# A gated linear-attention and token-mixing block: the last modulation vector summed by a chain of accumulating DMAs, two others folded into one matmul each, one projection reordered, a longer tail bank

## The chip, the cores and the metric

The kernel runs on one core of a Trainium2 chip. A core has five engines that run their own queues of instructions: TensorE (PE in the profile; its weight loads are PEld), VectorE (DVE), ScalarE (ACT), GpSimd (POOL) and SyncE (SP). DMAs are issued by an engine and carried by 16 DMA engines. The metric is the device time of one execution in microseconds. The kernel before takes 440.69 us, the median of three runs (440.43 to 441.95).

## The reference, cut to what matters

S = 2048 tokens, D = 448 channels, 16 heads of 28, F = 1792.

```python
mod = (silu(c) @ w_mod).reshape(1, 6, 1, D)
sa, ca, ga, sb, cb, gb = six vectors of mod          # j = 0 .. 5 in the kernel
h = layernorm(x) * (1 + ca) + sa
q, k, v = split(h @ wqkv);  phi(t) = where(t > 0, t + 1, exp(t)) + 1e-6
kv = sum over tokens of phi(k) v^T per head;  z = sum of phi(k)
o = (phi(q) kv) / (phi(q) z + 1e-6)
x = x + ga * (o @ wo)
h = layernorm(x) * (1 + cb) + sb
u = gelu(h^T @ w1 + b1);  y = (u @ w2 + b2)^T
x = x + gb * y
```

All is float32. The six modulation vectors are each a sum over the 448 inputs of c, held as 4 chunks of 112 rows (G = 112): vector j is the sum over the rows k of silu(c)[k] * w_mod[k, j*448:(j+1)*448], and it is used as a tile of 128 equal rows.

## The kernel before, in words

Everything is tiled by 128 tokens (16 tiles, t = 0 .. 15). Matmul operands in float32 are split into a high part, which the matmul takes exactly, and a low part; a product is then three matmuls (high by high, high by low, low by high), written into one accumulating bank of PSUM. The function `split` makes the two: ScalarE copies the high part (L79), VectorE subtracts (L80). In other places the low part is made by ScalarE, which writes the negative high part, and by an accumulating DMA on POOL, which adds the full value (L226, L404, L432, L257).

The order of every engine's work is written out by hand: the program order of the Python text is the order on each engine's queue, and semaphores make an instruction wait for its data or its buffer.

- **Stage A**, the loop over t = 3 .. 15 (L594): key projection of tile t (`project`, L356), transposes of tile t + 1 (L325), the outer products of tile t - 3 into four banks (`a_outer`, L453), and on the other engines the layer norm and its modulation (L307, L313), exponentials, phi and the splits of tiles ahead. Tiles 0 to 2 are done by hand ahead of the loop (L501 to L590). The query projection of tile 1, `project(1, 0, "qp", True)` (L582), sorts its eleven products by the key on L353, so that products with the low parts of the weight come late: high by high (3), low by high (3), low weights (3), then the two of the short fourth chunk. The low part of the first weight chunk is made by a DMA (`w_low_dma`, L226).
- **Between the stages** (L652 to L852): the sums, the products of kv with wo (L846), and the first splits of w1.
- **Stage B**, the loop over i = 0 .. 20 (L855): transposes of the normalised queries (L758), output projection (L778), residual, second layer norm, and from i = 5 the first products with w1 (`step`, L828 to L830). POOL makes small statistics there (L736, L792, L806, L811, L813, L818).
- **The last part** (from L1117): the remaining products with w1, gelu, and the products with w2 in a seven-product scheme (L1028, L1029); stores of the output.

The modulation vectors are made in three ways. Vectors 0 and 1 are done at the start and aren't touched here. Vectors 2, 4, 3 and 5 go through `load_mod` (four loads by SP), `mod_part` (VectorE multiplies a chunk by its column of silu(c) and adds it to an accumulator of 112 rows, L181 and L183; for vector 5 the first chunk is done by ScalarE, L179), `mod_split` (high and low part, 112 rows each), `mod_sum2` (two matmuls with a block of ones sum the rows and repeat the result in 128 rows, L199 and L200) and `mod_out` (ScalarE copies the bank out, L161). Their places: vector 2 has its products at t = 5 .. 8, the split at t = 9, the matmuls at t = 10 (L602), and it scales wo at t = 11 .. 14 (L611). Vector 4 has its products at t = 11 .. 14 and vector 3 at t = 15 and behind the loop; both are split at L670 and L671 and summed at L686 and L697. Vector 5 is loaded at i = 12 of stage B (L857), its products run at i = 13 .. 15, its matmuls stand at i = 16 (L868) and it is used from L945 and L1155 on.

At the very end, `mult7` leaves the last LAST = 2 row blocks of the last product out of their bank and hands them to `last7` (L1038), which multiplies them into a bank of its own (L1043) while VectorE adds the closed bank to the result (L1045); the last add takes the new bank, and SP stores the tile (L1046).

Buffers of 128 rows by 2 KB come from a pool of 76 (`slot`), and others from a pool of 25 that ends with stage B (`tslot`); a new tile waits for the last readers of the one whose buffer it gets.

Of the kernel before, what the change touches and what calls it, by code (L numbers as in the profile page):

```python
# [8 lines left out]
F32 = mybir.dt.float32  # L9
F32R = mybir.dt.float32r  # L10
AF = mybir.ActivationFunctionType
ALU = mybir.AluOpType
AX = mybir.AxisListType

P = 128
# [15 lines left out]
DVE_LOW = (0, 1, 13, 14, 15)  # L31
AHEAD = 8
LAG = 5
LAST = 2
PRE2 = {16: (1, 0), 12: (1, 1), 8: (1, 2), 3: (4, 3), 1: (4, 4)}
MOD_AT = {11: [(4, 0)], 12: [(4, 1)], 13: [(4, 2)], 14: [(4, 3)], 15: [(3, 0), (3, 1)]}
QS = {0: 2, 4: 2}
WARM = 9
ACT_STATS = ()
PRE = 9  # L40
# [7 lines left out]
def block_kernel(ctx: ExitStack, tc: tile.TileContext, x, wqkv, wo, w1, b1, w2, b2, c, wmod, out):  # L48
# [23 lines left out]
    def moving(new, name, dt=F32R, parts=P):  # L72
        return new(name, dt=dt, parts=parts, w=512)[:, 16:16 + D]

    def bank(name):
        return psum.tile([P, 512], F32, name=name, tag="bank")
# [32 lines left out]

    def load_mod(j):  # L110
        for k in range(4):
            wm[j, k] = (tslot if j == 5 else slot)(f"wm{j}_{k}", parts=G)
            nc.sync.dma_start(wm[j, k], wmod[k * G:(k + 1) * G, j * D:(j + 1) * D])

    raw_w = {}
# [38 lines left out]
    nc.vector.tensor_scalar_add(ec, ec, 1.0)  # L154
    nc.vector.reciprocal(ec, ec)
    nc.vector.tensor_mul(sc, ct, ec)
    mods, macc, part = {}, {}, {}

    def mod_out(j, ps):
        mods[j] = cst.tile([P, D], F32, name=f"mod{j}")  # L160
        nc.scalar.activation(mods[j], ps[:, :D], AF.Copy, bias=1.0 if j in (1, 4) else 0.0)  # L161
# [26 lines left out]
        return ps  # L188


    def mod_split(j):
        acc = macc.pop(j)
        macc[j] = (moving(slot, f"mh{j}", parts=G), moving(slot, f"ml{j}", parts=G))
        split(acc, *macc[j])

    def mod_sum2(j):
        ps = bank(f"modp{j}")
        hi, lo = macc.pop(j)
        nc.tensor.matmul(ps[:, :D], ones_r[:G, :], hi, start=True, stop=False)  # L199
        nc.tensor.matmul(ps[:, :D], ones_r[:G, :], lo, start=False, stop=True)  # L200
        return ps

    Whi, Wlo = {}, {}

# [31 lines left out]
    def load_to(i):  # L236
        while done["load"] < min(i, len(pieces)):
            k = done["load"]
            src, r, c0, n = pieces[k]
            raws[k] = slot(f"pr{k}", 4 * P)  # L240
            rows = 1 if n == 4 else 2
            nc.sync.dma_start(raws[k].rearrange("p (r c) -> p r c", r=rows),
                              src[r * P:(r + rows) * P, c0 * P:(c0 + n) * P].rearrange("(r p) c -> p r c", p=P))
            done["load"] += 1

    def split_to(i):
        while done["split"] < min(i, len(pieces)):
            k = done["split"]
            if k in TOKP:
                hi, lo = tslot(f"ph{k}", F32R, w=4 * P), tslot(f"pl{k}", F32R, w=4 * P)  # L250
            else:
                hi, lo = slot(f"ph{k}", 4 * P, F32R), slot(f"pl{k}", 4 * P, F32R)
            if k in PIECE_DMA:
                full = raws.pop(k)
                nc.scalar.activation(hi, full, AF.Copy)
                nc.scalar.activation(lo, hi.bitcast(F32), AF.Copy, scale=-1.0)
                nc.gpsimd.dma_start(lo, full, accum_op=ALU.add)  # L257
            else:
                split(raws.pop(k), hi, lo)
            parts[k] = (hi, lo)  # L260
            done["split"] += 1
# [81 lines left out]
    def project(t, j, name, late_low=False):  # L343
        hh, hl = heads[t]
        ps = bank(f"{name}{t}")
        o = ps[:, :D]
        todo = []
        for ch in range(4):
            a, b = (hh, ch, Whi[j, ch]), (hl, ch, Whi[j, ch])
            todo += [a, b] if ch == 3 else [a, (hh, ch, Wlo[j, ch]), b]  # L350
        if late_low:
            ws = [Wlo[j, ch] for ch in range(3)]
            key = lambda m: 3 if m[1] == 3 else 2 if any(m[2] is w for w in ws) else 0 if m[0] is hh else 1  # L353
            todo.sort(key=key)
        for n, (a, ch, b) in enumerate(todo):
            nc.tensor.matmul(o, a[:, ch * P:(ch + 1) * P], b, start=(n == 0), stop=(n == 10))  # L356
        return o
# [236 lines left out]
    for t in range(3, NT):  # L594
        kp = project(t, 1, "kp")
        if t + 1 < NT:
            a_transpose(t + 1)
        a_outer(t - KV_LAG)
        if t in Q_EARLY:
            a_q(t)  # L600
        if t == 10:
            mp = mod_sum2(2)  # L602
        if t + 1 < NT:
            a_split(t + 1)
        if t + 2 < NT:
            a_norm_a(t + 2)

        for j, i in MOD_AT.get(t, ()):
            mod_part(j, i)
        if 11 <= t < 15:  # L610
            nc.vector.tensor_mul(wo_sb[t - 11], wo_sb[t - 11], mods[2][:G])  # L611
        a_exp(t, kp)
        if t + 2 < NT:
            a_norm_b(t + 2)
        a_pk(t, kp)
        a_phi_q()
        a_pk_parts(t - 1)
        if t + 3 < NT:
            a_stats(t + 3)
        if t + 2 < NT:  # L620
            a_dup(t + 2)
        if t == 3:
            a_high(3)
            a_high(4)
        if t + 2 < NT:
            a_high(t + 2)
        if t == 10:
            mod_out(2, mp)
        if t + 4 < NT:
            load_x(t + 4)  # L630
        if 5 <= t < 9:
            mod_part(2, t - 5)
        if t == 9:
            mod_split(2)
        if 5 <= t <= 5 + QLATE:
            phi_q_sum(t - 5)
        if t in (10, 11):
            load_mod(14 - t)
        if t == 4:
            for g in range(4):  # L640
                w = tslot(f"wo{g}", parts=G)
                nc.sync.dma_start(w, wo[g * G:(g + 1) * G, :])
                wo_sb.append(w)
            load_qkv(2, tslot)
            b1c = cst.tile([P, NF], F32, name="b1c")
            nc.sync.dma_start(b1c, b1.rearrange("(k p) -> p k", p=P))
            b2c = cst.tile([P, NT], F32, name="b2c")
            nc.sync.dma_start(b2c, b2.rearrange("(k p) -> p k", p=P))
        load_to(PRE_LOAD.get(t, 0))
# [20 lines left out]
    mod_split(4)  # L670
    mod_split(3)  # L671
    load_to(14)
    split_to(4)
    zb = tslot("zb")
    nc.scalar.activation(zb, zp[:, :D], AF.Copy, bias=S * 1e-6)
# [18 lines left out]
    kvm = slot("kvm", parts=G)  # L694
    nc.vector.tensor_mul(kvm, kvb[:G, :D], mask)
    mod_out(4, mp)
    mp = mod_sum2(3)  # L697
    load_to(PRE + MID + 3)
    split_to(8)
# [144 lines left out]
    for g in range(4):  # L844
# [5 lines left out]
        Wph.append(hi)  # L850
        Wpl.append(lo)
    mod_out(3, mp)  # L852

    accs, early = None, []
    for i in range(NT + LAG):  # L855
        if i == NT - 4:
            load_mod(5)  # L857
        if NT - 3 <= i < NT:
            mod_part(5, i - NT + 3)
        if i < NT:  # L860
            b_transpose(i)
        if 0 <= i - 1 < NT:
            b_out(i - 1)
        nq = min(len(late), QS.get(i, 1))
        for _ in range(nq):
            a_q(late.pop(0))
        t = i - LAG
        mp = mod_sum2(5) if i == NT else None  # L868
        if t >= 0:
            if t == 0:  # L870
                accs = [bank(f"up{f}") for f in range(4)]
            if i > NT:
                if not early:
                    early = [bank(f"up{W1G[1][0] + f}") for f in range(W1G[1][1])]
                r = i - NT - 1
                step(NT + r, early, H2h[r], H2l[r], r == 0, False)
            step(t, accs, H2h[t], H2l[t], t == 0, t == NT - 1)
        if mp is not None:
            mod_out(5, mp)
        scale, res, norm1, norm2 = i + 1 < NT, 0 <= i - 2 < NT, 0 <= i - 3 < NT, 0 <= i - 4 < NT  # L880
        if i < NT:
            b_high(i)
        if res:
            b_res(i - 2)
        if scale:
            b_prod(i + 1)
        if norm2:
            b_norm2(i - 4, i)
        if res:
            b_mean1(i - 2, i)  # L890
        if norm1:
            b_norm1_a(i - 3)
        if scale:
            b_sum(i + 1)
        if norm1:
            b_norm1_b(i - 3, i)
        if scale:
            b_eps(i + 1)
        if i < NT:
            b_low(i)  # L900
        if norm1:
            b_mean2(i - 3, i)
        if scale:
            b_recip(i + 1)
        if scale:
            b_scale(i + 1)
        if scale:
            b_dup(i + 1)
        if norm2:
            b_low2(i - 4)  # L910
        a_phi_q(nq)
        load_to(14 + (i + 1) // 2)
        if res or norm1:
            b_rstd(i, 0 if res else 1, 2 if norm1 else 1)
        if i == NT - 1:
            mod_part(5, 3)
            mod_split(5)
        split_to(10 + (i + 1) // 2)


# [291 lines left out]
```

## Time and profile before

| | us |
|---|---|
| median of three runs | 440.69 |
| the profiled execution | 440.77 |
| its span, first to last instruction | 439.1 |
| busy time of POOL | 119.3 |
| software DMAs (POOL's queue), share of 16 engines | 23.8% |

The page gives the busy time of each engine, then the span in 40 slices of 11 us, the DMA queues, the chain of work that ended last, the costliest groups of instructions, and the DMA issues. Rows of the timeline give the start, the duration, the engine, the line, and in brackets how long the engine had been idle and what ended that. Two rows of the slices show how the load is spread (tenths busy):

```profile
DVE  5996898988898999997469586439999998898894
DMA  8987999993441224222427546476667977977531
```

VectorE is at nine tenths in many slices of the first half; the DMA engines are close to full in the first nine slices, which are stage A.

### The profile page before, as it was taken

How to read it: one execution, taken by the hardware profiler on the slowest of the kernel's cores; microseconds unless marked ns; L12 is line 12 of the kernel's file. 1: busy time of each engine (PE TensorE's matmuls, PEld its weight loads, DVE VectorE, ACT ScalarE, POOL GpSimd, SP SyncE). 2: the span in 40 equal slices, each digit the busy share in tenths (PEclk: the TensorE clock that was granted, in tenths of full speed). 3: DMA queues.
4: the chain of work that ended last, by engine and by line, in shares of the span. 5: the costliest groups of instructions: out<-in, count | busy, mean ns of one | idle time of the engine just before them, and what ended most of it. 6: DMA issues, size and time to landing. Idle time of an engine off the chain costs nothing.

```text
span 439.1 us, 7288 instructions
## 1 busy us (share of the span) xinstructions
PE 433.9 (99%) x2394; PEld 402.4 (92%) x2394; DVE 365.1 (83%) x792; ACT 266.9 (61%) x570; POOL 119.3 (27%) x196
## 2 busy tenths in 40 slices
PE   8999999999999999999999999999999999999996
PEld 7689999999899999999999999999999999999996
DVE  5996898988898999997469586439999998898894
ACT  3778877655657777776766254236675555655550
POOL 2205775520024455664300000010112230231110
PEclk9999999999999999999999999999999999999999
DMA  8987999993441224222427546476667977977531
GB/s 233 303 213 117 181 197 230 221 258 102 138 100 26 47 47 123 50 50 60 132 69 237 177 143 186 131 194 187 151 143 191 177 172 176 188 161 208 75 52 34
DMA packets 65022, 64.51 MB, mean 147 GB/s; under 512 B 8472, under 2 KB 56792, under 8 KB 64984
## 3 DMA queue, kind: packets, MB, share of 16 engines
q1 hardware_dynamic: 54608, 47.62, 36.8%
q0 software_dynamic: 10368, 16.42, 23.8%
q8 instruction: 19, 0.31, 0.3%
q14 instruction: 19, 0.16, 0.1%
q10 hardware_dynamic: 8, 0.00, 0.0%
HBM read 41.88 MB, written 7.34 MB: 112 GB/s over the span
## 4 chain that ended last, share of the span: by engine, by line
PE 95%; DMA 3%; DVE 1%; ACT 0%; issue 0%; SPq 0%; DVEq 0%
PE y L1028 19%; PE up L829 10%; PE up L828 10%; PE up L830 10%; PE y L1029 9%; PE op L778 8%; PE cacc L453 8%; PE qp L356 7%; PE kp L356 7%; DMA wl<-wr 2%; PE tq L758 2%; PE tp L325 1%; DMA wm<-in_w_mod_dram 1%; PE kvb L691 1%; PE wp L846 1%; PE colp L475 0%
## 5 line engine op out<-in xcount | busy, mean ns | idle before, releaser
L829 PE MATMUL up<-h2l,ph 128*128 128x448 f32 x224 | 81.3, 363 | 0.0
L828 PE MATMUL up<-h2h,ph 128*128 128x448 f32 x224 | 81.2, 362 | 0.0
L830 PE MATMUL up<-h2h,pl 128*128 128x448 f32 x224 | 80.7, 360 | 0.0
L988 POOL DMA_DIRECT2D a<-a x16 | 14.1, 948 | 145.5 <-DMA a<-in_B_w_dram 97.8
L828 PEld LDWEIGHTS up<-h2h,ph 128*128 128x128 f32 x224 | 42.0, 188 | 3.3
L830 PEld LDWEIGHTS up<-h2h,pl 128*128 128x128 f32 x224 | 41.9, 187 | 3.0
L829 PEld LDWEIGHTS up<-h2l,ph 128*128 128x128 f32 x224 | 42.0, 188 | 2.1
L80 DVE TENSOR_TENSOR pl<-pr,ph 128x512 fp32r<-128x512 f32 x48 | 32.3, 686 | 11.5 <-ACT ph L79 8.6
L79 ACT ACTIVATE ph<-pr 128x512 fp32r<-128x512 f32 x48 | 29.1, 627 | 17.8 <-PE up L829 7.4
L1050 ACT ACTIVATE cc<-y 128x448 f32<-128x448 f32 x24 | 13.0, 544 | 22.9 <-PE y L1029 22.9
L453 PE MATMUL cacc<-pkh,xh 128*128 128x448 f32 x64 | 24.3, 379 | 0.0
L453 PE MATMUL cacc<-pkl,xh 128*128 128x448 f32 x64 | 23.2, 363 | 0.0
L778 PE MATMUL op<-oh,pth 128*128 128x448 f32 x60 | 23.0, 383 | 0.0
L1071 POOL DMA_DIRECT2D out_dram<-yt x14 | 12.9, 921 | 34.9 <-DVE yt L1057 25.4
L778 PE MATMUL op<-oh,ptl 128*128 128x448 f32 x60 | 21.7, 362 | 0.0
L356 PE MATMUL qp<-wh,hh 128*128 128x448 f32 x60 | 21.6, 365 | 0.0
L356 PE MATMUL qp<-wh,hl 128*128 128x448 f32 x60 | 21.4, 362 | 0.0
L356 PE MATMUL kp<-wh,hl 128*128 128x448 f32 x56 | 20.3, 363 | 0.0
L356 PE MATMUL kp<-wh,hh 128*128 128x448 f32 x56 | 20.2, 362 | 0.0
L736 POOL TENSOR_SCALAR den<-den 128x16 f32<-128x16 f32 x16 | 8.6, 536 | 39.2 <-DVE den L733 39.1
L763 ACT ACTIVATE pth<-tq 128x512 fp32r<-128x512 f32 (+1 forms) x16 | 9.6, 599 | 15.7 <-PE tq L758 15.6
L302 POOL TENSOR_TENSOR rs<-ve,mhalf 128x1 f32<-128x1 f32 x16 | 13.9, 869 | 18.8 <-DVE ve L300 18.5
(234 smaller groups left out, 1356.9 us busy)
## 6 DMA issues: line engine op xcount, KB each, us to landing
pr<-in_B_w_dram SPq DMA_DIRECT2D x56, 256.0 KB, 2.9
a<-in_B_w_dram SPq DMA_DIRECT2D x32, 256.0 KB, 4.3
a<-in_B_w_dram SPq DMA_DIRECT2D x32, 192.0 KB, 4.2
wm<-in_w_mod_dram SPq DMA_DIRECT2D x24, 196.0 KB, 4.9
x<-in_A_x_dram SPq DMA_DIRECT2D x16, 224.0 KB, 4.0
out_dram<-x SPq DMA_DIRECT2D x14, 224.0 KB, 2.0
out_dram<-yt POOLq DMA_DIRECT2D x14, 224.0 KB, 4.5
pk<-pk POOLq DMA_DIRECT2D x12, 224.0 KB, 4.7
```

Source lines behind the costliest of these rows:

```text
L79: nc.scalar.activation(hi, full, AF.Copy)
L80: nc.vector.tensor_sub(lo, full, hi.bitcast(F32))
L302: nc.gpsimd.tensor_tensor(rs, ve, mhalf[:, 0:1], op=ALU.pow)
L356: nc.tensor.matmul(o, a[:, ch * P:(ch + 1) * P], b, start=(n == 0), stop=(n == 10))
L453: nc.tensor.matmul(cacc[ch][:, :D], a[:, s], b, start=(t == 0 and i == 0), stop=(t == NT - 1 and i == len(todo) - 1))
L778: nc.tensor.matmul(opb[t][:, :D], a[:, g * P:(g + 1) * P], b, start=(n == 0), stop=(n == len(todo) - 1))
L828: nc.tensor.matmul(ps[:, :D], hi[:, sl], mh, start=first, stop=False)
L829: nc.tensor.matmul(ps[:, :D], hi[:, sl], ml, start=False, stop=False)
L830: nc.tensor.matmul(ps[:, :D], lo[:, sl], mh, start=False, stop=last)
L988: nc.gpsimd.dma_start(w, a, accum_op=ALU.add)
L1028: nc.tensor.matmul(ps[:, :D], h[:, s], w, start=opens and r == r0, stop=False, skip_group_check=True)
L1029: nc.tensor.matmul(ps[:, :HD], l[:, s], wh, start=False, stop=closes and r == PAIRS - 1 - (LAST if (q, m) == (NP - 1, 6) else 0), skip_gro ...
```

## The change

- **Vector 5** is no longer summed by PE. Its four chunks are loaded at t = 12 of stage A into buffers of the pool of 76, scaled in place by ScalarE at t = 14 and 15, added to one chunk by three accumulating DMAs on POOL, and that chunk's 112 rows are folded onto themselves by seven more (112 to 56, 28, 14, 7, 4, 2 and 1 rows; `mod_fold`). The one row goes to DRAM by SP at i = 9 (`mod_row`) and comes back repeated in 128 rows at i = 10 (`mod_rows`). The products, the split, the two matmuls and the copy out of i = 12 .. 16 are gone.
- **Vectors 2 and 4** are folded before they are split: an accumulating DMA on POOL adds rows 64 to 111 of the accumulator to rows 0 to 47 (`fold`, at the end of t = 8 for vector 2, and at t = 14 for vector 4). High and low part of the 64 rows then lie in one tile of 128 rows, and one matmul with the ones sums both. For vector 2 the split moves from t = 9 to t = 10, the matmul and the copy out from t = 10 to 11, and the scalings of wo from t = 11 .. 14 to 12 .. 15.
- **The query projection of tile 1** takes the product with the low part of weight chunk 0 as the last of its eleven.
- **LAST** goes from 2 to 3.

```diff
-LAST = 2
+LAST = 3
+FOLD_AT = {3: 28, 4: 14, 5: 7, 6: 4, 7: 2}
+FOLDED = (2, 4)
...
+    def fold(j):
+        nc.gpsimd.dma_start(macc[j][:G - 64], macc[j][64:], accum_op=ALU.add)
+
     def mod_split(j):
         acc = macc.pop(j)
+        if j in FOLDED:
+            macc[j] = moving(slot, f"mb{j}")
+            split(acc[:64], macc[j][:64], macc[j][64:])
+            return
...
     def mod_sum2(j):
         ps = bank(f"modp{j}")
+        if j in FOLDED:
+            nc.tensor.matmul(ps[:, :D], ones_r, macc.pop(j), start=True, stop=True)
+            return ps
...
+    def mod_fold(j, n):
+        acc = macc[j]
+        h = (n + 1) // 2
+        nc.gpsimd.dma_start(acc[:n - h], acc[h:n], accum_op=ALU.add)
+
+    def mod_row(j):
+        mrow[j] = park.tile([1, D], F32, name=f"mrow{j}")
+        nc.sync.dma_start(mrow[j], macc.pop(j)[:1])
+
+    def mod_rows(j):
+        mods[j] = cst.tile([P, D], F32, name=f"mod{j}")
+        nc.sync.dma_start(mods[j], mrow[j].to_broadcast([P, D]))
...
-            key = lambda m: 3 if m[1] == 3 else 2 if any(m[2] is w for w in ws) else 0 if m[0] is hh else 1
+            key = lambda m: 3 if m[1] == 3 else 4 if m[2] is ws[0] else 2 if any(m[2] is w for w in ws) else 0 if m[0] is hh else 1
...
-        if t == 10:
+        if t == 11:
             mp = mod_sum2(2)
...
+        if t == 14:
+            fold(4)
-        if 11 <= t < 15:
-            nc.vector.tensor_mul(wo_sb[t - 11], wo_sb[t - 11], mods[2][:G])
+        if 12 <= t < 16:
+            nc.vector.tensor_mul(wo_sb[t - 12], wo_sb[t - 12], mods[2][:G])
...
-        if t == 10:
+        if t == 11:
             mod_out(2, mp)
...
-        if t == 9:
+        if t == 8:
+            fold(2)
+        if t == 10:
             mod_split(2)
...
+        if t == 12:
+            load_mod(5)
+        if t in (14, 15):
+            for k in (2 * t - 28, 2 * t - 27):
+                nc.scalar.activation(wm[5, k], wm[5, k], AF.Copy, scale=sc[:, k:k + 1])
+        if t == 15:
+            for k in range(2):
+                nc.gpsimd.dma_start(wm[5, k], wm[5, k + 2], accum_op=ALU.add)
...
     load_to(14)
+    nc.gpsimd.dma_start(wm[5, 0], wm[5, 1], accum_op=ALU.add)
+    macc[5] = wm[5, 0]
     split_to(4)
...
     mod_out(4, mp)
+    mod_fold(5, G)
...
     mod_out(3, mp)
+    mod_fold(5, 56)
...
     for i in range(NT + LAG):
-        if i == NT - 4:
-            load_mod(5)
-        if NT - 3 <= i < NT:
-            mod_part(5, i - NT + 3)
...
-        mp = mod_sum2(5) if i == NT else None
...
-        if mp is not None:
-            mod_out(5, mp)
...
+        if i in FOLD_AT:
+            mod_fold(5, FOLD_AT[i])
+        if i == 9:
+            mod_row(5)
+        if i == 10:
+            mod_rows(5)
...
-        if i == NT - 1:
-            mod_part(5, 3)
-            mod_split(5)
```

More of the change, by code (lines that the diff above doesn't have):

```diff
@@ L111, in load_mod @@
         for k in range(4):
-            wm[j, k] = (tslot if j == 5 else slot)(f"wm{j}_{k}", parts=G)
+            wm[j, k] = slot(f"wm{j}_{k}", parts=G)
             nc.sync.dma_start(wm[j, k], wmod[k * G:(k + 1) * G, j * D:(j + 1) * D])
@@ L156, in block_kernel @@
     nc.vector.tensor_mul(sc, ct, ec)
-    mods, macc, part = {}, {}, {}
+    mods, macc, part, mrow = {}, {}, {}, {}
     def mod_out(j, ps):
```

## The prediction

> **What bounds the kernel now.** I read the page's busy shares and chain first, then the matrix engine's timeline, then what ended each gap in it.
>
> ```profile
> span 439.1 us, 7288 instructions
> PE 433.9 (99%) x2394; PEld 402.4 (92%) x2394; DVE 365.1 (83%) x792; ACT 266.9 (61%) x570; POOL 119.3 (27%) x196
> PE 95%; DMA 3%; DVE 1%; ACT 0%; issue 0%; SPq 0%; DVEq 0%
> ```
>
> PE is the bound: 99% busy and 95% of the chain. Busy alone could mislead, because the ends of matmuls are modelled, so I go by starts. In the timeline a 448-column matmul follows the one before it 0.20 us later almost everywhere after 24 us. So the time is the sum of PE's starts plus the few places where the step is longer, plus a tail after the last matmul. An edit is worth what it takes from that sum, if nothing else becomes late.
>
> **The change part by part.** The whole sum is made against the profiled execution, 440.77 us (span 439.1, 1.67 around it); the median of the three runs shown is 440.69, so the two may be exchanged to 0.1 us.
>
> *Matmuls of the modulation vectors.* The rows are of PE's timeline at i = 16, where vector 5 is summed.
>
> ```profile
> 203.78 0.37 PE L199 MATMUL modp<-mh,ones_r 112*128 112x448 f32 x1
> 203.98 0.37 PE L200 MATMUL modp<-ml,ones_r 112*128 112x448 f32 x1
> 204.19 0.37 PE L828 MATMUL up<-h2h,ph 128*128 128x448 f32 x1
> ```
>
> Each takes 0.20 us of PE's order (203.98 - 203.78), the pair 0.41. Vector 5 loses both (0.41), vectors 2 and 4 one each (0.20 + 0.20). The one that stays has 128 rows in place of 112; the step of rows with 128 (204.19 and on) is 0.20 too. Sum: **0.81 us**.
>
> *q of tile 1.* Here is the one real stall after the start.
>
> ```profile
> 17.43 1.04 POOL L226 DMA_DIRECT2D wl<-wr  x1 [1.13 <-ACT wl L225]
> DMA to landing us min/median/max: 8.1/8.1/8.1
> 24.75 0.77 PE L356 MATMUL qp<-wh,hl 128*128 128x448 f32 x3
> 25.60 0.50 PEld L356 LDWEIGHTS qp<-wl,hh 128*128 128x128 f32 x3 [0.45 <-DMA wl<-wr]
> 25.60 0.88 PE L356 MATMUL qp<-wl,hh 128*128 128x448 f32 x3
> 26.31 0.36 PE L356 MATMUL qp<-wh,hh 128*128 128x448 f32 x1
> ```
>
> The low part of weight chunk 0 lands at 17.43 + 8.1 = 25.5. Its matmul could start at 24.75 + 3 x 0.20 = 25.35 and starts at 25.60 (0.25 lost); the three of the group then take 0.71 in place of 0.60 (0.11 lost). With that product last of the eleven, four matmuls stand before it (0.80), so it is wanted at 26.15, 0.6 after the landing. **0.36 us**; the other low operand of these eleven, hl, is already in use at 24.75, so nothing is late next there.
>
> *Tail bank of three.* The last two pairs of matmuls become the last three. A pair steps 0.31, its three halves 0.33 (434.60 to 434.94 in the timeline), so PE gains nothing. It is to let VectorE add the closed bank earlier.
>
> ```profile
> 433.24 0.62 DVE L1055 TENSOR_TENSOR cc<-y,cc 128x448 f32<-128x448 f32 x1 [0.65 <-PE y L1029]
> 433.90 0.82 DVE L1060 TENSOR_TENSOR xb<-cc,xb 128x224 f32<-128x224 f32 x2
> 434.50 0.26 PE L1029 MATMUL y<-ut,a22l 128*128 128x224 f32 x1
> 434.80 0.82 DVE L1045 TENSOR_TENSOR xb<-y,xb 128x224 f32<-128x224 f32 x2
> 435.16 0.28 PE L1043 MATMUL yl<-ut,a22l 128*128 128x224 f32 x1
> 435.72 0.39 DVE L1045 TENSOR_TENSOR xb<-yl,xb 128x224 f32<-128x224 f32 x1
> ```
>
> The bank closes at 434.76 and the add starts at 434.80. With three it closes 0.31 earlier, but VectorE is still at L1060 until 434.72 and the gap behind an add is 0.04: it can start at 434.76 at the earliest. So **0.04 us**, not 0.31; from there to the end VectorE is the chain (435.62, then 435.72), and PE's last matmul at 435.44 is not waited for.
>
> *Vector 5 by DMAs.* Taken away besides PE: one ScalarE product, three VectorE products, a split, an output copy. All lie beside PE, so nothing is booked. Added: four ScalarE copies in place at t = 14 and 15 (0.55 us each, as the 448-column row at 94.45 below), ten accumulating DMAs on POOL, two plain ones on SP, and the four loads moved to t = 12.
>
> ```profile
> 82.52 27.22 SPq L242 DMA_DIRECT2D pr<-in_B_w_dram  x17
> 94.45 0.55 ACT L363 ACTIVATE ek<-kp 128x448 f32<-128x448 f32 x1 [2.48 <-PE kp L356]
> 114.71 0.29 POOL L736 TENSOR_SCALAR den<-den 128x16 f32<-128x16 f32 x1 [23.05 <-DVE den L733]
> pk<-pk POOLq DMA_DIRECT2D x12, 224.0 KB, 4.7
> POOL vw L811 <- ACT sqb L285: 21.8, 16, 2.6
> ```
>
> The copies fit in ScalarE's 2.48 us of idle before 94.45. POOL is idle for 23 us before den at 114.71, and there the first three DMAs and the first fold wait for one another: the fold is issued two landings after the second DMA, so at 97.4 + 2 x 4.7 = 106.8, and POOL is free again 1 us later. At 8.1 a landing it is 114.6, and den, which PE's next transposes hang on, comes 0.9 late. I take 4.7, the median of twelve such transfers, and 0. In the next loop one fold of about 0.9 us of POOL stands in each of five steps ahead of L811, which waits 21.8 / 16 = 1.4 us for ScalarE there anyway: nothing, or 0.1 where that wait is shorter. The loads take the places of the first four of SP's seventeen, so the first piece of w1 is issued near 82.5 + 27.2 x 4/17 = 89 and lands near 94, ahead of its split (from 97 us; VectorE's half is the row at 99.17 below): nothing. SP's row copy and broadcast queue ahead of loads that are used several steps later: nothing. **0 us**.
>
> *Folds and steps moved.* Vector 2: its fold goes on POOL at the end of t = 8, its split (one ScalarE copy, one VectorE subtract) from t = 9 to 10, its output copy and the four scalings of wo one step later. ScalarE at t = 10 loses the copy out and gains the copy of the split. VectorE gains 0.62 at t = 10 and has one 0.62 scaling less done from t = 11 on. Vector 4's fold waits on POOL for VectorE's last product at t = 14; behind it stands one accumulate of pk, whose sum is wanted 9 us later. **0 us**, if POOL has room at t = 8; that is the first rival.
>
> Sum: 0.81 + 0.36 + 0.04 = 1.2 us, 440.77 - 1.2 = **439.6**.
>
> **The rivals.**
>
> *POOL's queue is full at t = 8 (slower than before).*
>
> ```profile
> 63.37 0.86 POOL L432 DMA_DIRECT2D pkl<-pk  x1 [0.57 <-ACT pkl L431]
> DMA to landing us min/median/max: 6.7/6.7/6.7
> 64.51 0.84 POOL L438 DMA_DIRECT2D pk<-pk  x1 [0.28 <-issue]
> DMA to landing us min/median/max: 6.6/6.6/6.6
> 66.85 0.88 POOL L404 DMA_DIRECT2D xl<-h  x1 [0.89 <-ACT rk L364]
> 67.24 0.58 ACT L431 ACTIVATE pkl<-pkh 128x448 fp32r<-128x448 f32 x1
> 70.37 0.87 POOL L432 DMA_DIRECT2D pkl<-pk  x1 [2.64 <-ACT mh L79]
> 71.47 0.86 POOL L438 DMA_DIRECT2D pk<-pk  x1 [0.23 <-DVE hl L80]
> 72.03 0.89 POOL L302 TENSOR_TENSOR rs<-ve,mhalf 128x1 f32<-128x1 f32 x1
> 72.95 0.68 DVE L313 SCALAR_TENSOR_TENSOR h<-h,rs,mod 128x448 f32<-128x448 f32 x1 [0.91 <-POOL rs L302]
> 74.84 0.49 PE L325 MATMUL tp<-ident,h 128*128 128x128 f32 x3
> ```
>
> The data for 70.37 are ready at 67.82, yet it is issued 0.3 after the transfer of 63.37 lands (70.07), with two others under way; 71.47 follows the landing of 71.11 in the same way. POOL seems to hold three such accumulates at a time. If a fold of 48 rows counts as one, it takes the place at 70.37; pkl goes to 71.4, the next pk behind the third landing (about 73.1) to 73.4, and rs, behind it, ends at 74.8 in place of 72.92. VectorE waits for rs and ends h at 75.5; PE wants it at 74.84 - 0.36 - 0.41 = 74.07 and stands 1.45. PE is then 0.7 late, 0.9 with vector 2's matmul, and 0.65 is won later: 440.77 + 0.25 = **441.0**. It decides from the point where three full accumulates and a fold do not fit; with room in proportion to rows, 3.4 places are needed where the rows show at least 3 and fewer than 4. I lean to room, for 48 rows are well under half a transfer.
>
> *VectorE gives it back.*
>
> ```profile
> 76.10:89.70 13.60, 13.60 (x74) 12.66 (x73) 13.25 (x28) 9.07 (x20) 8.00 (x10) 1.00 1.05 234
> 155.70:201.80 46.10, 46.10 (x248) 42.90 (x247) 44.81 (x107) 34.97 (x74) 28.37 (x58) 1.00 0.29 70
> 89.00 0.26 ACT L317 ACTIVATE h<-h 128x64 f32<-128x64 f32 x1 [1.27 <-DVE h L313]
> 89.40 0.60 PE L325 MATMUL tp<-ident,h 128*128 128x128 f32 x4
> ```
>
> In both stretches VectorE (third figure) works 97% of the time. At 89.40 the fourth transpose comes 0.47 after its input (89.73 against 89.26). PE's gain by then, 0.36 + 0.20 = 0.56, would be cut to the margin unless VectorE moves too. For the forecast: both stretches begin behind a wait for ScalarE that follows PE, and a scaling has left the first. If VectorE stays, the 0.56 goes and 0.65 less little remains: **440.2**.
>
> *A buffer is handed on too early (slower).* The buffers of vector 5's third and fourth chunk are free when its first two accumulates land, and by a count in the code the pool is then at its fullest, 71 of 76 before and 73 after. If the w1 split at 98 to 100 us gets them, it waits, and the sums for zp wait behind it.
>
> ```profile
> 99.17 1.28 DVE L80 TENSOR_TENSOR pl<-pr,ph 128x512 fp32r<-128x512 f32 x2
> 105.24 0.37 PE L669 MATMUL zp<-zh,ones_r 128*128 128x448 f32 x1
> ```
>
> From that split's second half to zp lie two 0.65, three adds of 0.65 and a split of 1.2, some 4.5 us; zp is wanted near 104.7, so any landing after 100.2 costs. Issued at 97.4, a 4.7 landing makes 1.9 (**441.5**), one of 8.1 makes 5.3 (444.9). The Trainium skill ("DMA: Bandwidth & Descriptors", section "Anatomy of one DMA — SWDGE (gpsimd) path") gives about 2.0 us plus bytes over 436 GB/s for such a DMA: for 196 KB an estimate of 2.5, landed at 99.9, no wait and 439.6. The trace does not agree: its twelve took 4.7 in the median.
>
> *The tail brings its full 0.31*, or another small stall goes: **439.3**.
>
> **How the numbers follow.** Forecast 0.57 (its own range 439.2 to 440.1, for a tenth or two lost to longer landings near 70 us), queue full 0.19, VectorE 0.13, buffer 0.06, larger gain 0.05. The likeliest gives 439.6. The range 439.1 to 441.5 takes in all but the buffer's long end, a queue that costs more than worked out, and the extremes. What a measurement of this kernel can tell from no change is about 0.5%, 2.2 us: faster by more means under 438.5, which no case reaches (0.04 for what I have not seen); slower by more means over 442.9: the buffer's long end and a doubled queue, 0.06. Same: 0.90.
>
> **What would show it.** Right: no DMA-ended weight load near 25.6; one modp matmul at about 77 and 107, two at 111, none near 204; the last L1045 still 0.1 behind the one before. Wrong: POOL's L432 or L302 near 70 to 74 later than now and VectorE's L313 waiting over 2 us (queue); transposes that wait for h near 79 to 90 (VectorE); L80 behind a DMA near 99 (buffer); POOL's L736 ended by a fold. The prediction fails outright if a chain of folds outlasts 114 us or the broadcast vector comes after 206.

## The result, and the profile after

The changed kernel takes 447.91 us, the median of five runs (447.39 to 448.77), against 441.15 us (440.43 to 441.95): a ratio of 1.0157 (95% interval 1.0144 to 1.0171). It is 6.8 us slower, where 1.2 us faster was forecast with a range up to 441.5.

First the page of the changed kernel (busy times, the granted clock in 40 slices of 11.1 us, the chain that ended last by engine):

```profile
span 445.9 us, 7315 instructions
PE 437.0 (98%) x2391; PEld 404.5 (91%) x2391; DVE 362.7 (81%) x788; ACT 267.9 (60%) x571; POOL 128.1 (29%) x208
PEclk9999999999699999999999999999999999999999
PE 88%; issue 4%; DVE 3%; DMA 3%; POOL 2%; ACT 0%; POOLq 0%; DVEq 0%
```

PE was 95% of the chain and is 88%. Time between issues (4%) and POOL (2%) have entered it, VectorE has gone from 1% to 3%, and the 3% of DMAs, which had been transfers of the start, are now `wm<-wm`. In one slice, the eleventh, the granted clock of PE falls to six tenths. The chain in order of time shows the place (start, length, what):

```profile
97.88 5.79 DMA wm<-wm
103.67 3.15 issue
106.83 6.50 DMA wm<-wm
...
113.45 0.64 DVE cs L719
114.08 0.04 issue
114.13 4.82 PE kvb L730 x24
```

Two of vector 5's accumulating DMAs stand in it, one behind the other, and what comes after them is no use of vector 5 but `cs`, a copy of the sums that PE needs for kvb. The timeline of VectorE and of PE there:

```profile
106.08 1.29 DVE L82 TENSOR_TENSOR pl<-pr,ph 128x512 fp32r<-128x512 f32 x2
113.45 1.16 DVE L719 COPY cs<-cacc 128x448 f32<-128x448 f32 x2 [6.08 <-DMA wm<-wm]
```

```profile
109.09 0.95 PE L730 MATMUL kvb<-cs,wr 128*112 128x112 f32 x8
114.13 4.82 PE L730 MATMUL kvb<-cs,wr 128*112 128x112 f32 x24 [4.09 <-DVE cs L719]
118.63 0.66 PE L211 MATMUL modp<-mh,ones_r 112*128 112x448 f32 x1
119.13 0.37 PE L212 MATMUL modp<-ml,ones_r 112*128 112x448 f32 x1
```

In the kernel before, the copies waited for nothing and the 32 matmuls followed one another:

```profile
105.83 1.15 DVE L680 COPY cs<-cacc 128x448 f32<-128x448 f32 x2
108.26 3.31 PE L691 MATMUL kvb<-cs,wr 128*112 128x112 f32 x32
```

Now VectorE stands 6.08 us for a DMA whose data it does not read. `cs` of the second bank was given the buffer of vector 5's chunk 1, and the third accumulating DMA (L710, issued at 106.83) reads that chunk until it lands at 113.33. PE stands 4.09 us behind it. When it goes on, the 24 small matmuls take 4.5 us from start to start (114.13 to 118.63, 0.19 each), where the first ones step 0.10. The windows (PE busy is the second figure, the granted clock the one behind POOL) say why:

```profile
108.00:112.00 4.00, 2.04 (x15) 1.76 (x13) 0.00 (x0) 3.50 (x8) 0.00 (x0) 1.00 0.99 264
112.00:116.00 4.00, 1.87 (x10) 1.88 (x11) 2.55 (x5) 0.63 (x1) 0.88 (x1) 0.53 0.37 100
116.00:120.00 4.00, 4.00 (x22) 3.91 (x22) 1.89 (x4) 0.63 (x1) 0.00 (x0) 0.61 0.26 70
120.00:124.00 4.00, 4.00 (x16) 2.67 (x15) 3.51 (x8) 1.09 (x2) 1.14 (x2) 1.00 0.01 1
```

The granted clock is 0.50 from 112.3 to 119.1 us: it falls while PE stands, and after the standstill PE runs at half its clock until it has worked some 5 us.

Why did the third DMA take 6.5 us? The waits of SP's queue and its timeline in that place show another buffer of the chain that was handed on:

```profile
SPq L267 <- DMA wm<-wm: 4.0, 1, 4.0
```

```profile
106.25 1.75 SPq L267 DMA_DIRECT2D pr<-in_B_w_dram  x4
```

Chunk 3's buffer went to a load of w1. SP's queue stood 4.0 us behind it, until the second DMA, which reads chunk 3, had landed (106.20), and then sent four loads of 256 KB at once, just as the third DMA was issued.

A second, smaller loss is at 90 us. These are weight loads, ScalarE, VectorE and SP of the changed kernel:

```profile
90.16 0.19 PEld L478 LDWEIGHTS cacc<-pkl,xh 128*128 128x128 f32 x1 [0.35 <-DMA pkl<-pk]
92.62 0.19 PEld L381 LDWEIGHTS kp<-wh,hh 128*128 128x128 f32 x1 [0.55 <-ACT hh L81]
93.34 0.19 PEld L381 LDWEIGHTS kp<-wh,hl 128*128 128x128 f32 x1 [0.43 <-DVE hl L82]
```

```profile
91.97 0.60 ACT L81 ACTIVATE hh<-tp 128x512 fp32r<-128x512 f32 x1 [2.34 <-DMA pk<-pk]
```

```profile
76.60 6.88 SPq L115 DMA_DIRECT2D wm<-in_w_mod_dram  x5
```

The last four of these five loads are vector 5's, issued at 81.6 to 83.1 us. The low part of pk of tile 12 and the sum of pk behind it, issued at 83.2 and 83.8, take 6.9 and 8.1 us to land, where they took 5.6 and 6.2 before. PE waits for the first; the buffer of the second is wanted for `hh` of tile 15, and ScalarE stands 2.34 us for it.

Third, at 70 us, and last the tail:

```profile
70.21 0.19 PEld L478 LDWEIGHTS cacc<-pkl,xh 128*128 128x128 f32 x1 [0.38 <-DMA pkl<-pk]
```

```profile
440.98 0.82 DVE L1097 TENSOR_TENSOR xb<-cc,xb 128x224 f32<-128x224 f32 x2
441.72 0.81 DVE L1082 TENSOR_TENSOR xb<-y,xb 128x224 f32<-128x224 f32 x2
442.63 0.39 DVE L1082 TENSOR_TENSOR xb<-yl,xb 128x224 f32<-128x224 f32 x1
```

Setting the start of each PE instruction after against the same one before gives the account (us, plus is later):

| where | changes by |
|---|---|
| up to 23 us (varies between executions, from -0.1 to +0.8 in the others) | +0.18 |
| q of tile 1 | -0.36 |
| pk of tile 7, landing at 70.17 | +0.28 |
| vector 2, one matmul for two | -0.21 |
| 89.6 to 93.7 us | +1.12 |
| vector 4, one matmul for two | -0.18 |
| wait of `cs` for the DMA | +4.25 |
| half clock after it | +2.42 |
| vector 5's two matmuls gone | -0.41 |
| tail | -0.17 |
| sum | +6.9 |

The spans differ by 6.8. Each gain that was forecast is there. They are outweighed by two waits that vector 5's DMAs cause, and by the clock.

### The profile page after: what moved, and what is told of

It reads as the page before. It is cut to its first block, busy times and chain, and to the rows that moved or that the text cites. A ratio compares the mean times of both kernels' runs of the same rounds, so it can differ in the third digit from the quotient of the medians.

```text
span 445.9 us, 7315 instructions
## 1 busy us (share of the span) xinstructions
PE 437.0 (98%) x2391; PEld 404.5 (91%) x2391; DVE 362.7 (81%) x788; ACT 267.9 (60%) x571; POOL 128.1 (29%) x208
## 4 chain that ended last, share of the span: by engine, by line
PE 88%; issue 4%; DVE 3%; DMA 3%; POOL 2%; ACT 0%; POOLq 0%; DVEq 0%
PE y L1065 18%; PE up L870 10%; PE up L869 10%; PE up L868 10%; PE y L1066 9%; PE op L818 8%; PE qp L381 6%; PE kp L381 4%; PE cacc L478 3%; DMA wm<-wm 3%; PE tq L798 2%; PE warm L145 1%; PE kvb L730 1%; PE tp L350 1%; PE kp L527 1%
## 5 line engine op out<-in xcount | busy, mean ns | idle before, releaser
L982 DVE TENSOR_TENSOR u<-u,mod 128x448 f32<-128x448 f32 x14 | 8.7, 620 | 13.2 <-ACT u L981 13.0
```

## The experiments

Each time is set against the kernel before on the same chip; its median was 440.8 to 440.9 us in these groups.

**Vector 5 back on PE.** All else as changed.

```diff
-        if t == 12:
-            load_mod(5)
...
+        if i == NT - 4:
+            load_mod(5)
+        if NT - 3 <= i < NT:
+            mod_part(5, i - NT + 3)
...
+        mp = mod_sum2(5) if i == NT else None
```

> The changed kernel with vector 5 summed as before (its products on VectorE, two matmuls at i = 16), all else as changed. Buffer theory (all of the loss comes from vector 5's DMAs: its buffers are handed on too early, and its loads stand in the way at 90 us): no wait of the cs copies near 107 us, kvb matmuls 0.10 us apart, no stall at 89.6 to 93.7; the two folds, the q order and the longer tail bank keep 0.4 + 0.36 + 0.16 us less what the pkl landing at 70.1 us takes back (0.36): 0.4 to 0.9 us below the kernel before. Rival (the folds of vectors 2 and 4 on POOL's queue, or the moved scalings, carry part of the loss): 1 us or more above the kernel before.

Measured 440.68 us, a ratio of 0.9994 (0.9976 to 1.0012). The wait of `cs`, the low clock and the stalls at 90 us are gone, so the whole loss comes with vector 5's DMAs. The expected gain of 0.4 to 0.9 us did not come: the 0.2 us here cannot be told from nothing. The profiled execution began 0.8 us late and gave 0.5 back at 70 us.

**Only vector 5's DMAs, on the kernel before.**

```diff
-            wm[j, k] = (tslot if j == 5 else slot)(f"wm{j}_{k}", parts=G)
+            wm[j, k] = slot(f"wm{j}_{k}", parts=G)
...
+        if t == 12:
+            load_mod(5)
```

> The kernel before with vector 5's DMAs alone (no folds of vectors 2 and 4, old q order, old tail bank). Buffer theory: the buffer of chunk 1 goes by the order of releases to the low part of a split of w1 ahead of the cs copies on VectorE, so the same DMA (landing near 113 us) holds them up: 6 to 8 us above the kernel before, with the low clock after the wait. Rival (it takes the folds or the moved steps to bring the loss): within 1 us of the kernel before.

Measured 443.70 us, a ratio of 1.0052 (1.0033 to 1.0071). The mechanism came as expected and the size did not. A split of w1 got the buffer:

```profile
111.05 0.69 DVE L81 TENSOR_TENSOR pl<-pr,ph 128x512 fp32r<-128x512 f32 x1 [2.56 <-DMA wm<-wm]
```

```profile
112.33 2.61 PE L715 MATMUL kvb<-cs,wr 128*112 128x112 f32 x24 [1.59 <-DVE cs L704]
```

```profile
112.00:116.00 4.00, 3.67 (x30) 3.60 (x31) 4.00 (x8) 1.89 (x4) 0.11 (x1) 1.00 0.79 208
```

Here the third DMA landed after 4.1 us (110.86) in place of 6.5, PE stood 1.59 us, and its clock stayed at 1.00: the same 24 matmuls step 0.10. Another 1.8 us are lost in PE's waits between 91 and 107 us, most of them behind late DMAs.

**The buffers held.** POOL writes a few elements of chunks 1 to 3 at i = 2, so their buffers come free only then.

```diff
+        if i == 2:
+            for k in range(1, 4):
+                nc.gpsimd.memset(wm[5, k][:1, :8], 0.0)
```

> The changed kernel, but the buffers of vector 5's chunks 1 to 3 stay taken until i = 2 of stage B (POOL writes a few elements there), so no copy or split gets them while DMAs read them. Buffer theory: the cs copies start at about 107 us with no wait for a DMA, the kvb matmuls follow one another by 0.10 us, and 4.3 us of stall and 2.4 us of low clock go: 6.3 to 6.8 us below the changed kernel, with the 1.1 us lost at 89.6 to 93.7 us still there, so 0 to 0.8 us above the kernel before. Rival (contention: the three long transfers and the w1 loads beside them are what is late): the wait near 107 us stays or moves to another copy, and the time stays within 1 us of the changed kernel.

Measured 440.87 us, a ratio of 1.0007 (0.9992 to 1.0022): 7 us below the changed kernel.

```profile
106.93 1.15 DVE L719 COPY cs<-cacc 128x448 f32<-128x448 f32 x2
```

```profile
108.73 3.31 PE L730 MATMUL kvb<-cs,wr 128*112 128x112 f32 x32
111.80 0.45 PE L211 MATMUL modp<-mh,ones_r 112*128 112x448 f32 x1
```

The copies wait for nothing, and all 32 matmuls run in 3.07 us (108.73 to 111.80). The DMAs, their order and their bytes are the same, and the third lands at 110.2, 3 us after the copies have begun, so it is the buffer. The stall at 90 us is still there (ScalarE's `hh` waits 2.22 us for the DMA).

**PE kept busy in the wait.** Nineteen matmuls that nobody reads stand where PE waits; the wait itself is left.

```diff
     for ch in range(4):
+        if ch == 1:
+            for _ in range(19):
+                nc.tensor.matmul(cacc[0][:, :D], ones_r, zs[0], start=True, stop=True)
         for g in range(4):
```

> The changed kernel with 19 matmuls of 448 columns, whose result nobody reads, put on PE between the first and the second row block of the sums for kvb, where PE stands and waits for the copy. Clock theory (the granted clock of 0.53 at 112 to 116 us follows from PE's 4.1 us of standing still): the wait for the DMA stays, but the kvb matmuls after it follow one another by 0.10 us in place of 0.19, and the time is 2.0 to 2.5 us below the changed kernel. Rival (the kvb matmuls are slow for a reason of their own, such as operands or the DMA traffic): 0.19 us apart as now, time unchanged within 0.5 us.

Measured 444.80 us, 3.1 below the changed kernel.

```profile
109.81 4.09 PE L730 MATMUL cacc<-zh,ones_r 128*128 128x448 f32 x19
113.73 2.52 PE L733 MATMUL kvb<-cs,wr 128*112 128x112 f32 x24
116.02 0.45 PE L211 MATMUL modp<-mh,ones_r 112*128 112x448 f32 x1
```

The 24 matmuls now take 2.29 us (113.73 to 116.02) in place of 4.50, so the half clock is the price of standing still. In this execution the DMA also landed 1.2 us earlier (112.1), but PE gained only 0.4 by it: the nineteen matmuls held it until 113.73, some 0.85 us after the first copy was done (begun at 112.20, 0.64 long).

**hh of tile 15 elsewhere**, on top of the held buffers.

```diff
-        hh = slot(f"hh{t}", 512, F32R)
+        hh = tslot(f"hh{t}", F32R, w=512) if t == NT - 1 else slot(f"hh{t}", 512, F32R)
```

> The kernel with held buffers, and the high part of the transposed h of tile 15 in the other pool, where it gets a buffer that nobody has used, in place of that of pk of tile 11, which an accumulating DMA reads until 91.5 us. Hand-on theory for the 0.8 us lost at 92 to 93.7 us: ScalarE makes the part near 90.1 us with no wait for a DMA, and 0.6 to 0.8 us of PE's loss there go; the 0.3 us at 89.8 us (pkl of tile 12 landing late) stay. Rival (the loss there comes from the slower transfers alone): ScalarE's wait ends no earlier, or another wait of the same length takes its place.

Measured 440.36 us, a ratio of 0.9991 (0.9977 to 1.0005), 0.5 below the run with held buffers, which is within the noise of the two; the trace says more.

```profile
90.38 0.60 ACT L81 ACTIVATE hh<-tp 128x512 fp32r<-128x512 f32 x1
```

```profile
92.20 0.69 DVE L82 TENSOR_TENSOR hl<-tp,hh 128x512 fp32r<-128x512 f32 x1 [1.25 <-DMA pk<-pk]
```

ScalarE waits no more. The low part now got the buffer in question and waits for the same DMA, a little less late: of the 0.8 us there, 0.28 are left. The sum of pk takes 7.9 us to land (8.0 with held buffers), so ScalarE's wait was the hand-on. The 0.3 us at 89.8 us, which were expected to stay, are not there: PE had lost 0.76 us at 70 us in this execution and came after that landing. How much of the rest is owed to PE's coming later, one execution cannot tell.

**No loads of vector 5**, on top of the held buffers.

```diff
-            nc.sync.dma_start(wm[j, k], wmod[k * G:(k + 1) * G, j * D:(j + 1) * D])
+            if j < 5:
+                nc.sync.dma_start(wm[j, k], wmod[k * G:(k + 1) * G, j * D:(j + 1) * D])
...
-                nc.scalar.activation(wm[5, k], wm[5, k], AF.Copy, scale=sc[:, k:k + 1])
+                nc.scalar.activation(wm[5, k], mods[1][:G], AF.Copy, scale=sc[:, k:k + 1])
```

> The kernel with held buffers, without the four loads of vector 5 (196 KB each, issued at 81.6 to 83.1 us): the scalings read another tile instead, so that the sum for vector 5 is not computed. Contention theory for the late landings near 90 us: with this traffic gone the low part of pk of tile 12, issued near 83, lands near 88.8 as in the kernel before, the sum of pk behind it near 90, and PE has no stall at 89.6 to 93.7; about 1 us below the run with held buffers. Rival (the fold of vector 4 and the order on POOL's queue make these landings late): they stay at 89.8 and 91.5 us.

Measured 439.52 us, a ratio of 0.9970 (0.9960 to 0.9980), for a kernel that leaves out the sum for vector 5. The two DMAs of 83 us land after 5.1 and 6.2 us (6.8 and 8.0 with held buffers and the loads, 5.6 and 6.2 in the kernel before), and there is no stall at 90 us. The buffers' order shifted too (`hh` of tile 15 got another one), so the late landing is shown to be the loads' and the wait of `hh` is the two together: a late DMA, and a buffer that hangs on it.

**q of tile 1 alone**, on the kernel before.

```diff
-key = lambda m: 3 if m[1] == 3 else 2 if any(...)
+key = lambda m: 3 if m[1] == 3 else 4 if m[2] is ws[0] else 2 if any(...)
```

> The kernel before with the order of q of tile 1 alone changed. Landing theory (the 0.36 us won at 25.6 us are given back where PE waits for the low part of pk of tile 7, whose landing at 69.5 to 71.1 us in the profiles so far goes by the transfers and not by PE): the step at 25.6 us is gone, a wait for that DMA of 0.2 to 0.5 us stands near 70 us in its place, and the time is within 0.2 us of the kernel before. Rival (the gain is kept, as the prediction had it): no wait over 0.1 us near 70 us, 0.3 to 0.4 us below.

Measured 440.66 us, a ratio of 0.9998 (0.9989 to 1.0006). The profile speaks for the rival and the time for neither: in the profiled execution the DMA landed at 69.38, PE did not wait at 70 us and kept its 0.36. But in the ten profiles in which that DMA is made, it lands between 69.4 and 71.1 us; PE waits 0.3 to 0.9 us for it in five, and under 0.1 in the other five, the kernel before among them. The gain is kept in some executions and given back in others.

**The chain in stage B**, and then the low part of pk of tile 7 made by VectorE besides.

```diff
+        if i == 2:
+            load_mod(5)
...
+        if 4 <= i < 8:
+            k = (0, 2, 1, 3)[i - 4]
+            nc.scalar.activation(wm[5, k], wm[5, k], AF.Copy, scale=sc[:, k:k + 1])
...
+FOLD_AT = {10: 112, 11: 56, 12: 28, 13: 14, 14: 7, 15: 4, 16: 2}
```

> The changed kernel with vector 5's whole chain moved into stage B: loads at i = 2, one scaling on ScalarE at each of i = 4 to 7, the three accumulating DMAs at i = 6, 8 and 9, the seven folds at i = 10 to 16, the row out and back at i = 17 and 18. Buffer theory (the chain itself is free where buffers are plentiful and nobody waits for one; by a count in the code 53 to 57 of the 76 are taken in stage B): no wait for a DMA of vector 5, no stall at 89.6 to 93.7 us, PE 0.41 us less than with vector 5 on PE; 0.6 to 1.3 us below the kernel before. Rival (a chain of ten DMAs on POOL costs by itself, behind its statistics in stage B): PE stalls of 0.3 us or more between 130 and 210 us, and a time at or above the kernel before.

```diff
-PK_LOW = (9,)
+PK_LOW = (7, 9)
```

> As the run with the chain in stage B, and the low part of pk of tile 7 made by VectorE in place of an accumulating DMA. Theory (what q of tile 1 wins at 25.6 us is given back at 70.1 us, where PE waits for that DMA to land): no wait at 70 us, and one transfer less in the full stretch; 0.1 to 0.5 us below the run without it. Rival (VectorE has no room at t = 8, and its own late results take the place of the DMA): transposes or weight loads that wait for VectorE between 65 and 75 us, same time or more.

The first gave 441.49 us, a ratio of 1.0017 (1.0008 to 1.0026): the rival by its time and its stalls, though the longest stall comes from ScalarE and not from POOL. No buffer is waited for, but the last scaling meets a stretch in which nothing has room:

```profile
155.57 0.65 ACT L929 ACTIVATE wm<-wm,sc 112x448 f32<-112x448 f32 x1
156.13 0.52 ACT L399 ACTIVATE eq<-qp 128x448 f32<-128x448 f32 x1
156.56 0.52 ACT L400 ACTIVATE rq<-qp 128x448 f32<-128x448 f32 x1
157.11 0.63 DVE L405 SCALAR_TENSOR_TENSOR pq<-eq,rq 128x448 f32<-128x448 f32 x1 [1.33 <-ACT rq L400]
```

```profile
162.11 0.63 PE L787 MATMUL tq<-ident,pn 128*128 128x128 f32 x4 [0.65 <-DVE pn L772]
```

The scaling stands ahead of eq and rq on ScalarE, VectorE waits 1.33 us for rq, and PE is 0.8 us later by 162. From there every step is 0.1 us longer until 198 us, with an accumulating DMA on POOL in each. That these cause it is not shown: in the last run below they stand in the same loop until 169 us, and no step there is longer. The second gave 440.80 us, a ratio of 1.0002 (0.9994 to 1.0011): 0.7 below the first, no wait at 70 us, PE 0.9 us earlier than before at 107 us, and all of that lost at 161 to 198 us in the same way.

**The chain between the stages**, with pk of tile 7 by VectorE: loads behind the fourteenth load of w1, scalings ahead of the splits of wp, where ScalarE is idle.

```diff
     load_to(14)
+    load_mod(5)
     split_to(4)
...
     split_to(8)
+    for k in (0, 2, 1, 3):
+        nc.scalar.activation(wm[5, k], wm[5, k], AF.Copy, scale=sc[:, k:k + 1])
...
         fn(0)
+    for k in range(2):
+        nc.gpsimd.dma_start(wm[5, k], wm[5, k + 2], accum_op=ALU.add)
```

> The changed kernel with vector 5's chain moved out of both full stretches: loads behind the fourteenth load of w1 (near 104 us), the four scalings on ScalarE ahead of the splits of wp (near 112 us), the first two accumulating DMAs at about 115 us behind POOL's den, the third at i = 0 of stage B, the folds at i = 1 to 7, the row out and back at i = 9 and 10; and the low part of pk of tile 7 by VectorE. Theory (the chain costs nothing where no buffer it reads is wanted, no DMA in the full stretch stands beside its loads, and ScalarE and POOL have room): no wait of a copy for these DMAs, no stall at 70 and at 89 to 94 us, no VectorE-bound steps from 160 us on; PE 1.2 to 1.5 us earlier than before at 205 us, 1.0 to 1.7 us below the kernel before. Rival (PE that comes 0.9 us earlier into stage B runs into VectorE there, as VectorE is 97% busy from 156 to 202 us): transposes of the normalised queries wait for VectorE, 0 to 0.6 us below the kernel before.

Measured 440.42 us, a ratio of 0.9988 (0.9978 to 0.9998). The profiled execution took 439.49, as the theory had it, but the runs spread from 439.39 to 441.71. Then the accumulating DMAs were moved behind the rows of wp:

```diff
-    for k in range(2):
-        nc.gpsimd.dma_start(wm[5, k], wm[5, k + 2], accum_op=ALU.add)
...
+        if i == 1:
+            for k in range(2):
+                nc.gpsimd.dma_start(wm[5, k], wm[5, k + 2], accum_op=ALU.add)
```

> The run with the chain between the stages, but its first two accumulating DMAs wait until i = 1 of stage B, the third until i = 2, the folds go at i = 3 to 9, the row out and back at i = 11 and 12. In the run before, the two stood beside the rows of the products with wo that SP sends from 114.7 us on: the last of these landed at 128.3 us, where the kernel before has them down at 126 to 127, and PE stood 0.16 us at 128.4. Theory (in its slower executions, up to 2 us above its fastest, this wait is what grows): no wait of PE near 128 us, 1.0 to 1.6 us below the kernel before in the median, with less spread. Rival (the spread comes from elsewhere, such as the start, or two more steps of folds meet VectorE's full stretch after 156 us): median 0.3 to 0.7 us below as in that run.

Measured 439.70 us (439.33 to 440.23 in twelve runs), a ratio of 0.9971 (0.9960 to 0.9983): 1.2 us below the kernel before, the best of all and faster than both kernels. The last of the rows lands at 125.6 us and PE has no wait near 128. That the slower runs of the version before it waited there is argued, for none of them was profiled; what is shown is that with the DMAs moved they are gone. The trace of this last version has the terms of the forecast (0.36 us for q of tile 1, 0.2 each for vectors 2 and 4, 0.41 for vector 5), and the low part of pk of tile 7 on VectorE besides. That its median is 1.2 us below, the number forecast, is no support for the kernel that was forecast, whose chain stood elsewhere. A buffer of the chain is handed on early here too: SP's queue stands 6.0 us for one of the accumulating DMAs (until 129.9) ahead of a load of w1. It costs nothing, for that load then waits for another buffer until 148.3. The page of this run:

```profile
span 437.6 us, 7310 instructions
PE 432.9 (99%) x2391; PEld 402.2 (92%) x2391; DVE 363.6 (83%) x789; ACT 267.0 (61%) x570; POOL 128.5 (29%) x207
PEclk9999999999999999999999999999999999999999
```

## Why the prediction was wrong, point by point

- **The step that failed** is the one that booked vector 5's DMAs at "0 us", and with it the rival "A buffer is handed on too early" at a chance of 0.06. The mechanism in that rival is the one that happened. Its place, its price and its chance were wrong:
  - It looked at chunks 2 and 3 (its third and fourth; they are counted from 0 here), free when the first two DMAs land, and at the w1 split near 99 us. No engine waited for chunk 2's buffer, free from the landing at 103.7. Chunk 3's held up the loads of w1. The harm came from chunk 1, which the third DMA reads. The prediction had that DMA's end in hand, for the sake of POOL's `den` (the fold behind it at 106.8 us by two landings of 4.7, at 113.6 by 8.1; it was issued at 113.67), but never asked who gets the buffer that it reads.
  - Of the two landings in its sum it took the median of twelve, 4.7. The three measured 5.8, 7.7 and 6.5, beside loads of w1. For the third, six profiles side by side: with no load issued within 2 us of it, 3.5 to 4.2 us in four (hh of tile 15 elsewhere, held buffers, vector 5 alone, no loads of vector 5); with three, 5.6 (PE kept busy); with four, 6.5. That the loads are the cause is argued from these six, not tried by itself. The Trainium skill ("DMA: Bandwidth & Descriptors", section "Anatomy of one DMA — SWDGE (gpsimd) path") would have given an estimate of 2.5, as that rival quotes it; the three whole-chunk DMAs took 3.5 us or more in every run that has them.
  - It priced a wait as the wait alone. Of the 6.7 us here, 2.4 are the clock after it. The Trainium skill ("TensorE: Matmul & The Clock Gate", section "Part 1: The HAM clock gate (the "warmup" mystery)") says that PE falls to half its rate after an idle window of about 3.4 us; the runs agree in part: 4.09 us of standing still gave 0.53 to 0.61, 1.59 us gave 1.00. But the clock fell at 112.3, some 2.2 us after the end of PE's last matmul (110.04), so how long a standstill it takes is not shown here.
- **The loads at t = 12** were booked at nothing, because the split of w1 that they push back still has its data in time. That was right, and not the only thing they touch: they ran beside two accumulating DMAs that PE and ScalarE waited for next (+1.12; gone without the loads).
- **q of tile 1** gave its 0.36 at 25.6 us. "Nothing is late next there" was too short a look: the next thing late is the landing at 70 us, whose margin in the kernel before was less than nothing (PE waited 0.08), and which takes back up to all of it.
- **Matmuls of the modulation vectors**: 0.81 forecast, 0.41 + 0.21 + 0.18 = 0.80 measured.
- **Tail**: 0.04 forecast, 0.17 measured. The mechanism was right (VectorE bounds it), the floor was not: the second add starts 0.08 before the end of the two before it, not 0.04 after.
- **POOL's queue full at t = 8** did not come. POOL's rows after:

```profile
67.12 0.88 POOL L429 DMA_DIRECT2D xl<-h  x1 [1.32 <-ACT pkh L452]
67.71 1.16 POOL L194 DMA_DIRECT2D acc<-acc  x1
70.48 0.91 POOL L457 DMA_DIRECT2D pkl<-pk  x1 [1.61 <-issue]
...
72.18 0.87 POOL L327 TENSOR_TENSOR rs<-ve,mhalf 128x1 f32<-128x1 f32 x1
```

  The fold was issued with three full ones under way (of 63.20, 64.38 and 67.12). The next pkl followed the first landing (70.17) by 0.3 as before, with the fold still under way, and `rs` starts at 72.18 in place of 72.03: a fold of 48 rows does not use up the place of a full transfer.
- **VectorE gives it back** did not come either: in the best version PE is 0.77 us earlier than before at 107 us and 1.19 at 203, behind both of VectorE's full stretches. Where the second stretch did become late, with the chain in stage B, the first 0.8 us follow a scaling added to ScalarE; what made its later steps longer is open.

## What to carry to other kernels

A DMA that reads or writes a buffer keeps it until it lands, and the next owner may be a tile that has nothing to do with it: where a chain of DMAs is moved into a full stretch, list for each buffer of the chain the last transfer that touches it, its latest landing, and who gets the buffer next. Price a stall of PE of 4 us with the matmuls behind it at half clock. And a chain that is off the critical path is free only where its loads, its buffers and its engines all have room. Here that was with its loads and scalings between the stages and its DMAs behind the next burst of row copies; with the loads in the stage before, or the scalings in the loop after, it was not.

## What had not been expected of the hardware

PE after 4.09 us of standing still ran 24 matmuls of 112 columns at 0.19 us each, and at 0.10 when it was kept busy with matmuls that nobody reads. These saved 2.2 us there, and being a few too many held PE 0.85 us longer than the copy did. Accumulating DMAs of 196 KB within the core took 3.5 us at the least and up to 7.7 beside loads and one another, and beside four loads of 196 KB two other accumulating DMAs took 1.3 and 1.9 us longer. With a fold of 48 rows among them, POOL issued a fourth accumulating DMA while three were under way; in the traces without that fold there were never more than three.
